# Sigmoid attention and GELU feed-forward on one core: four score tiles of a unit pair shared by VectorE and ScalarE in halves

## The chip, the cores and the metric

The kernel runs on one core of a Trainium2 chip. The metric is the device time of one launch in microseconds (us), of which three runs were made before the change. Five things work side by side on a core: TensorE (PE in the profile; its weight loads are listed apart as PEld), VectorE (DVE), ScalarE (ACT), GpSimd (POOL) and the DMA queues, most of which SyncE (SP) issues. TensorE can only write to PSUM, a small memory of eight banks; ScalarE or VectorE has to carry its results from there into SBUF before a bank can take the next ones.

## The reference

All of it is float32. Eight batches (B), twelve heads, 448 positions (S), head size 64; then a feed-forward network over the 3584 tokens with 768 and 2048 features:

```python
scores = scale * np.matmul(q, k.transpose(0, 1, 3, 2)) - np.log(S)
attn = 1.0 / (1.0 + np.exp(-scores))           # sigmoid, no softmax
x = np.matmul(attn, v)                          # then (B*S, heads*head size)
h = x @ w_in
g = 0.5 * h * (1.0 + erf(h * inv_sqrt2))
out = g @ w_out
```

## The kernel before

The first 240 us are the attention, the rest is the feed-forward network, a long unbroken row of matmuls (line L726). The change lies in the attention alone.

**Units and tiles.** The work is cut into 24 units of two head pairs (p = 0, 1) each. For each head pair the 448 keys are three full chunks of 128 (c = 0, 1, 2) and a tail of 64. A score tile (u, p, c) holds 128 keys against 448 queries for the two heads of a pair (j = 0, 1): 128 partitions by 2 x 448 numbers, each head's 448 in a PSUM bank of its own. The four PSUM places of two banks each (`ps0` to `ps3` in `place`, the order `perm`) are used in turn, so score tile n + 4 writes where score tile n was. For precision each operand is split in a high and a low float32r part (`hi`, `lo`), and a score tile takes three products (lo with hi, hi with lo, hi with hi) for two heads, six matmuls that run two at a time.

**Units in pairs.** Units 2 to 17 are done two at a time, in eight calls of `paired(u)`. Such a call first makes twelve score tiles, n = 0 to 11: 0 to 5 are those of unit u, 6 to 11 those of unit u + 1. ScalarE takes a tile out of PSUM with the sigmoid on the way (`sigmoid`, L455, 896 numbers in each partition). For n = 3 and n = 7 VectorE copies the raw scores out instead (`evict`, L459), and ScalarE does the sigmoid later, in SBUF, behind tiles 8 and 11 (`late_sigmoid`, L463). Between these copies VectorE rounds the last operand of the pair to its high part in front of tile 3 (`high_qk`, L436) and takes its low part behind tile 3 (`split_qk`, L446); tiles 9 to 11 are the first to need it.

**Values.** Then `values` multiplies the probabilities of unit u with v into a place of PSUM (`pav`, L516), tail first, then the chunks in the order of a list, once for each half of the 128 keys. In between, VectorE reads two columns of it (`mark`, L543) and TensorE makes the tail scores of the next unit (`sc_t`, L500). The same follows for unit u + 1. `park` (L575 and others) takes each result out of PSUM. VectorE and ScalarE also decode the feed-forward weights in the time between (L149, L160, L179, L187, L193).

**What sets the order.** Each engine works through its own instructions in the order in which the code above issues them; nothing is sorted anew. The tile framework adds the semaphore waits by itself, from which instruction writes or reads which tile: a matmul waits until its place in PSUM has been read, a read until its matmuls are done.

Of the kernel before, what the change touches and what calls it, by code (L numbers as in the profile page):

```python
# [14 lines left out]
AF = mybir.ActivationFunctionType  # L15
# [7 lines left out]
def tile_sigmoid_attention_gelu_ffn(  # L23
# [10 lines left out]
    nc = tc.nc  # L34
# [7 lines left out]
    FULL = S // P  # L42
# [5 lines left out]
    SCALE = 1.0 / math.sqrt(D)  # L48
    NEG_LOG_S = -math.log(S)
# [63 lines left out]
    def weight_pair(n, name):  # L113
        return sb.tile([P, 2, WU], F32R, tag=f"whl{n % 2}", name=name, bufs=WHL // 2)
# [227 lines left out]
    def rows(j):  # L342
        return slice(j * D, j * D + D)
# [20 lines left out]
    def braid(m):  # L364
        return m.rearrange("p (a b) -> p b a", a=2)
# [14 lines left out]
    def attention(at, ps):  # L380
        raws, vals, parts, probs, pavs = {}, {}, {}, {}, {}
        total = B * NU
        SINGLE = PAIRED[-1] + 2
        loaded, rounded = set(), set()
        own = at.tile([P, 8, 2, S], F32, name="a_all", bufs=1)
        lent = [wst_all[:, n * 2 * S : (n + 1) * 2 * S] for n in range(3)]
        for n in range(2):
            m = weight_pair(1, f"a_lent{n}").bitcast(F32)
# [4 lines left out]
        def occupy(u, p, c):  # L393
            slot = next(s for s in vacant if s[0] or u < SINGLE)
            vacant[:] = [s for s in vacant if s is not slot]
            probs[u, p, c] = slot
            return slot[1]

        def vacate(u, p, c):
            vacant.append(probs.pop((u, p, c)))  # L400
# [47 lines left out]
        def ordered(a):  # L448
            return a.rearrange("p j (a b) -> p j a b", a=2)

        def sigmoid(u, p, c, sc, braided):
            a = to = occupy(u, p, c)
            if braided:
                to, sc = ordered(a), sc.rearrange("p j (b a) -> p j a b", a=2)
            nc.scalar.activation(to, sc, AF.Sigmoid, bias=NEG_LOG_S, scale=SCALE)  # L455

        def evict(u, p, c, sc):
            a = occupy(u, p, c)
            nc.vector.tensor_copy(ordered(a), sc.rearrange("p j (b a) -> p j a b", a=2))  # L459

        def late_sigmoid(u, p, c):
            a = probs[u, p, c][1]
            nc.scalar.activation(a, a, AF.Sigmoid, bias=NEG_LOG_S, scale=SCALE)  # L463

        def place(i, name):
            return ps[max(i - 1, 0)].tile([P, 2, 512], F32, tag=f"ps{i}", name=name)[:, :, :S]

        def scores(u, p, c, i, finish=sigmoid):
            sc = place(i, f"sc{u}_{p}_{c}")
            keys = slice(c * P, c * P + P)  # L470
            braided = (u, p) in parts
            if braided:
                hi, lo = parts[u, p]
                terms = ((hi, lo), (lo, hi), (hi, hi))
            else:
                terms = ((raws[u][:, p],) * 2,)
            last = len(terms) - 1
            for n, (ks, qs) in enumerate(terms):
                for j in range(2):
                    nc.tensor.matmul(  # L480
                        sc[:, j],
                        ks[rows(j), 1, keys],
                        braid(qs[rows(j), 0]) if braided else qs[rows(j), 0],
                        start=n == 0,
                        stop=n == last,
                    )
            if finish is sigmoid:
                sigmoid(u, p, c, sc, braided)
            else:
                finish(u, p, c, sc)  # L490
# [18 lines left out]
        def values(u, i, tail, order, meanwhile, idle):  # L509
            pav = pavs[u] = place(i, f"pav{u}")  # L510

            def chunk(c, swap):
                a = [probs[u, 0 if c == FULL else p, c][1] for p in range(2)]
                for p, j in QUARTERS:
                    half = rows(p ^ swap)
                    nc.tensor.matmul(  # L516
                        pav[rows(j), p],
                        vals[u][half, p, j, c],
                        a[p][half, j],
                        start=not swap and c == order[0],  # L520
                        stop=c == (order[-1], FULL - 1)[swap],
                        skip_group_check=True,
                    )

            if u == total - 1:
                chunk(FULL, 0)
                for p in range(2):
                    for c in range(FULL):
                        for j in range(2):
                            nc.tensor.matmul(  # L530
                                pav[rows(j), p],
                                vals[u][:, p, j, c],
                                probs[u, p, c][1][:, j],
                                start=False,
                                stop=c == FULL - 1,
                                skip_group_check=True,
                            )
                meanwhile()
                return
            for c in order:  # L540
                chunk(c, 0)
            vacate(u, 0, FULL)
            nc.vector.tensor_copy(mark, pav[:, :, 0])  # L543
            meanwhile()
            scores_tail(u + 1, tail)
            idle()
            for c in range(FULL):
                chunk(c, 1)
            for p in range(2):
                for c in range(FULL):  # L550
                    vacate(u, p, c)
# [3 lines left out]
        def park(u):  # L555
            b, n = divmod(u, NU)
            pav = pavs[u]
            if b < 2:
# [13 lines left out]
                return  # L572
            if u < SINGLE:
                x = on_way[u % 2][:, :2]
# [17 lines left out]
        perm = (0, 1, 3, 2)  # L592
# [9 lines left out]
        def single(u):  # L602
# [11 lines left out]
            first, second = PAIRED[-1], PAIRED[-1] + 1  # L614
            if u == SINGLE:
                keep()
                dec.round(first - 2)
            if u == SINGLE + 1:
                nc.vector.tensor_tensor(x01, x11, x01, op=ALU.subtract)

            def meanwhile():
# [3 lines left out]
                if u + 1 == PAIRED[0]:  # L625
                    split_qk(u + 2, 0)
                if u == SINGLE:
                    dec.join(second - 2)
                    dec.round(second - 2)
                if u == SINGLE + 1:  # L630
                    nc.vector.tensor_tensor(kept["x6"], x01, x00, op=ALU.add)
# [22 lines left out]
        def paired(u):  # L654
            a, b, c, d = perm
            first, second = u - PAIRED[0], u + 1 - PAIRED[0]
            begun = first > 0
            after = [(u + 2, 0), (u + 2, 1)]
            if u + 2 < SINGLE:
                after.append((u + 3, 0))  # L660
            load(u + 3)
            load_v(u + 2)
            tiles = [(w, p, c) for w in (u, u + 1) for p in range(2) for c in range(FULL)]
            for n, at_tile in enumerate(tiles):
                if n == FULL:
                    high_qk(u + 1, 1, nc.vector.tensor_copy)
                scores(*at_tile, perm[n % 4], evict if n in (3, 7) else sigmoid)
                if n == 3:
                    split_qk(u + 1, 1)
                if n in (8, 11):  # L670
                    late_sigmoid(*tiles[{8: 3, 11: 7}[n]])
            part_tiles(*after[0])
            for w, p in after[1::-1]:
                high_qk(w, p, nc.gpsimd.tensor_copy)
            if begun:
                dec.round(first - 2)
                dec.join(second - 2)
                split_qk(*after[0])

            def idle1():  # L680
                load(u + 4)
                if begun:
                    dec.round(second - 2)
                    dec.post()
                else:
                    split_qk(*after[0])
                dec.scale(first)
                dec.place(first)

            values(u, a, b, [FULL, 1, 2, 0], lambda: None, idle1)  # L690
            park(u)
            load_v(u + 3)
            for w, p in after[2:]:
                high_qk(w, p, nc.gpsimd.tensor_copy)
            split_qk(*after[1])

            def idle2():
                load(u + 5)
                for w, p in after[2:]:
                    split_qk(w, p)  # L700
                dec.join(first)
                dec.scale(second)
                dec.place(second)

            values(u + 1, c, d, [0, 1, 2, FULL], lambda: None, idle2)
            park(u + 1)

        u = 0
        while u < total:
            if u in PAIRED:  # L710
                paired(u)
                a, b, c, d = perm
                perm = (b, a, d, c)
                u += 2
            else:
                single(u)
                a, b, c, d = perm
                perm = (a, b, d, c)
# [345 lines left out]
```

## Time and profile before

| | us |
|---|---|
| median of three runs (lowest, highest) | 1010.02 (1009.84, 1010.33) |
| the profiled execution | 1008.94 |
| its span, first to last instruction | 1007.0 |
| busy in the span: PE / PEld / DVE / ACT / POOL | 1002.7 / 903.0 / 719.9 / 666.0 / 127.3 |
| granted TensorE clock, share of full speed | 1.000 |

The profiled execution lies 1.94 us above its own span and 1.08 us below the median. Matmuls are pipelined, and a matmul's end in the profile is modelled: two that follow each other overlap in the list, and PE is called busy also where it came late. How far TensorE is from its own pace is seen from the distance between the starts of its matmuls, not from its busy share.

### The profile page before, as it was taken

Reading aid. Unit: us, or ns where it says so; the run is one execution under the profiler, and the core shown is the slowest. Engines: PE = TensorE matmul, PEld = TensorE weight load, DVE = VectorE, ACT = ScalarE, POOL = GpSimd, SP = SyncE. Lnnn points to the kernel's source line nnn. Section 1 sums busy time; section 2 is a strip of 40 time slices with the busy share of each in tenths; the row PEclk is TensorE's granted clock in tenths of the full one; section 3 lists DMA queues with packets and bytes.
Section 4 is the critical chain, followed back from the end, with each engine's and each line's share of the span. In section 5 each row is a group of like instructions: output and inputs, shape, how many; then the busy total and the mean of one; then the engine's idle time right before and its main releaser. Section 6 shows DMA issues by size and latency. Waiting matters only on the chain.

```text
span 1007.0 us, 16532 instructions
## 1 busy us (share of the span) xinstructions
PE 1002.7 (100%) x6406; PEld 903.0 (90%) x6406; DVE 719.9 (71%) x822; ACT 666.0 (66%) x920; POOL 127.3 (13%) x177
## 2 busy tenths in 40 slices
PE   9999999999999999999999999999999999999998
PEld 5655565567999999999999999999999999999998
DVE  3598888787988986764378877535887774378873
ACT  5787788688886766467565655766656467665652
POOL 0244444133223300010000000100000000000000
PEclk9999999999999999999999999999999999999999
DMA  9999999998997665563434546534444543334441
GB/s 247 276 278 339 361 343 346 358 321 271 344 327 215 206 219 154 168 210 132 137 110 128 151 138 183 190 110 138 126 117 147 166 150 112 112 110 126 145 142 59
DMA packets 82990, 199.16 MB, mean 198 GB/s; under 512 B 9184, under 2 KB 33984, under 8 KB 82912
## 3 DMA queue, kind: packets, MB, share of 16 engines
q1 hardware_dynamic: 69360, 152.24, 49.2%
q0 software_dynamic: 11616, 39.23, 11.4%
q10 hardware_dynamic: 1936, 6.63, 2.0%
q8 instruction: 50, 0.82, 0.3%
q14 instruction: 28, 0.23, 0.1%
HBM read 156.10 MB, written 41.29 MB: 196 GB/s over the span
## 4 chain that ended last, share of the span: by engine, by line
PE 100%; DVE 0%; ACT 0%; issue 0%
PE pf L726 76%; PE pav L516 12%; PE sc L480 9%; PE sc_t L500 2%; PE pav L530 0%; PE warm L595 0%; DVE tmp L974 0%; ACT y L975 0%
## 5 line engine op out<-in xcount | busy, mean ns | idle before, releaser
L726 PE MATMUL pf<-op,whl 128*128 128x448 f32 x2016 | 382.1, 352 | 0.0
L726 PEld LDWEIGHTS pf<-op,whl 128*128 128x128 f32 x2016 | 380.9, 189 | 0.5
L726 PE MATMUL pf<-xh_p,whl 128*128 128x448 f32 x1296 | 352.7, 353 | 0.0
L329 DVE TENSOR_TENSOR whl<-wst_all,whl 128x768 fp32r<-128x768 f32 x224 | 213.5, 954 | 153.6 <-ACT whl L322 153.2
L322 ACT CAST whl<-wst_all 128x768 fp32r<-128x768 f32 x224 | 186.0, 830 | 142.4 <-PE pf L726 124.6
L726 PEld LDWEIGHTS pf<-xh_p,whl 128*128 128x128 f32 x1296 | 244.9, 189 | 1.0 <-issue 0.7
L726 PE MATMUL pf<-xl_p,whl 128*128 128x448 f32 x624 | 219.9, 352 | 0.0
L763 DVE TENSOR_TENSOR op<-g,op 128x896 fp32r<-128x896 f32 x112 | 121.3, 1083 | 0.9 <-ACT op L773 0.9
L726 PEld LDWEIGHTS pf<-xl_p,whl 128*128 128x128 f32 x624 | 117.9, 189 | 0.1
L773 ACT CAST op<-g 128x896 fp32r<-128x896 f32 x112 | 104.8, 936 | 1.7 <-PE pf L726 1.7
L516 PE MATMUL pav<-a_all,v 64*64 64x448 f32 x936 | 104.5, 540 | 0.0
L455 ACT ACTIVATE a_all<-sc 128x896 f32<-128x896 f32 x91 | 77.0, 937 | 15.1 <-PE sc L480 15.1
L516 PEld LDWEIGHTS pav<-a_all,v 64*64 64x64 f32 x936 | 38.9, 132 | 47.4 <-issue 36.7
L763 DVE TENSOR_TENSOR g<-g,g 128x896 f32<-128x896 f32 x64 | 69.3, 1083 | 0.0
L760 ACT ACTIVATE g<-tmp 128x448 f32<-128x448 f32 x64 | 40.3, 631 | 37.8 <-DVE tmp L763 37.7
L760 ACT ACTIVATE g<-pf 128x448 f32<-128x448 f32 x64 | 34.8, 543 | 39.8 <-PE pf L726 39.6
L354 POOL DMA_DIRECT2D x<-scr_x x24 | 18.3, 816 | 324.5 <-ACT g L870 204.0
L763 DVE TENSOR_TENSOR tmp<-pf,g 128x448 f32<-128x448 f32 x64 | 39.7, 622 | 26.2 <-PE pf L726 16.6
L480 PE MATMUL sc<-lo,hi 64*128 64x448 f32 x276 | 52.5, 371 | 0.0
L446 DVE TENSOR_TENSOR lo<-qk,hi 128x896 fp32r<-128x896 f32 x46 | 51.1, 1112 | 0.9 <-POOL hi L436 0.3
L480 PE MATMUL sc<-hi,lo 64*128 64x448 f32 x276 | 49.5, 349 | 0.0
L480 PE MATMUL sc<-hi 64*128 64x448 f32 x276 | 49.5, 349 | 0.0
(87 smaller groups left out, 917.9 us busy)
## 6 DMA issues: line engine op xcount, KB each, us to landing
wst_all<-scr_in SPq DMA_DIRECT2D x112, 384.0 KB, 3.0
wst_all<-scr_out SPq DMA_DIRECT2D x112, 384.0 KB, 3.1
v<-v_dram SPq DMA_DIRECT2D x48, 256.0 KB, 10.4
raw<-w_in_dram SPq DMA_DIRECT2D x16, 767.8 KB, 8.9
out_dram<-tmp SPq DMA_DIRECT2D x47, 224.0 KB, 2.1
qk<-q_dram SPq DMA_DIRECT2D x23, 448.0 KB, 9.6
qk<-k_dram SPq DMA_DIRECT2D x46, 224.0 KB, 10.0
scr_out<-wd POOLq DMA_DIRECT2D x36, 256.0 KB, 5.0
```

What stands on the lines that cost most here:

```text
L322: nc.scalar.copy(hl[:, 0], t)
L329: nc.vector.tensor_tensor(hl[:, 1], t, hl[:, 0], op=ALU.subtract)
L354: queue.dma_start(dst[:, :, a], src[:, :, a])
L446: nc.vector.tensor_tensor(lo, raw, hi, op=ALU.subtract)
L455: nc.scalar.activation(to, sc, AF.Sigmoid, bias=NEG_LOG_S, scale=SCALE)
L480: nc.tensor.matmul(sc[:, j], ks[rows(j), 1, keys], braid(qs[rows(j), 0]) if braided else qs[rows(j), 0], start=n == 0, stop=n == last,)
L500: nc.tensor.matmul(sc[rows(p), j], raw[rows(j), p, 1, FULL * P :], raw[rows(j), p, 0], start=True, stop=True,)
L516: nc.tensor.matmul(pav[rows(j), p], vals[u][half, p, j, c], a[p][half, j], start=not swap and c == order[0], stop=c == (order[-1], FULL - ...
L726: nc.tensor.matmul(bank, a, braid(m), **flags)
L760: nc.scalar.activation(straight(dst), unbraid(src), AF.Gelu)
L763: nc.vector.tensor_tensor(out, a, b, op=op)
L773: nc.scalar.copy(op[:, 0], src)
```

## The change

In a pair, tiles 1, 3, 5 and 7 are now handled by a new function, `share`, instead of tiles 3 and 7 by `evict`. ScalarE does the sigmoid of the first head's half (448 numbers) straight from PSUM, VectorE copies the second head's half out raw, and `late_sigmoid` does only that half. The late halves of tiles 1, 3 and 5 stand behind tile 8, that of tile 7 behind tile 11. In the first `values` of a pair the chunks come in the order tail, 1, 0, 2 instead of tail, 1, 2, 0.

```diff
+        SHARED = {8: (1, 3, 5), 11: (7,)}
...
-        def evict(u, p, c, sc):
-            a = occupy(u, p, c)
-            nc.vector.tensor_copy(ordered(a), sc.rearrange("p j (b a) -> p j a b", a=2))
+        def share(u, p, c, sc):
+            a = ordered(occupy(u, p, c))
+            sc = sc.rearrange("p j (b a) -> p j a b", a=2)
+            nc.scalar.activation(a[:, 0], sc[:, 0], AF.Sigmoid, bias=NEG_LOG_S, scale=SCALE)
+            nc.vector.tensor_copy(a[:, 1], sc[:, 1])
 
         def late_sigmoid(u, p, c):
-            a = probs[u, p, c][1]
+            a = probs[u, p, c][1][:, 1]
             nc.scalar.activation(a, a, AF.Sigmoid, bias=NEG_LOG_S, scale=SCALE)
...
-                scores(*at_tile, perm[n % 4], evict if n in (3, 7) else sigmoid)
+                scores(*at_tile, perm[n % 4], share if n in SHARED[11] + SHARED[8] else sigmoid)
                 if n == 3:
                     split_qk(u + 1, 1)
-                if n in (8, 11):
-                    late_sigmoid(*tiles[{8: 3, 11: 7}[n]])
+                for m in SHARED.get(n, ()):
+                    late_sigmoid(*tiles[m])
...
-            values(u, a, b, [FULL, 1, 2, 0], lambda: None, idle1)
+            values(u, a, b, [FULL, 1, 0, 2], lambda: None, idle1)
```

VectorE's queue in the fourth pair (units 8 and 9) from `park` of the unit before to the first piece of weight decoding behind the copies (L193), with the semaphores that each instruction waits for. A score tile is named sc, unit, p, c, so `sc8_1_0` is tile 3 of this pair and `sc9_0_1` is tile 7. Before:

```order
L575 COPY h1_x_130<-pav7_1005 128x896 [waits PE_49]
L436 CAST hi9_1_1081<-qk9_796 128x896 [waits PE_49]
L459 COPY a_all_126<-sc8_1_0_1084 128x896 [waits PE_49]
L446 TENSOR_TENSOR lo9_1_1082<-qk9_796,hi9_1_1081 128x896 [waits DVE_49]
L459 COPY wst_all_109<-sc9_0_1_1117 128x896 [waits PE_49]
L193 ISA wd4_1034<-raw4_730,wd4_1034 128x1536
```

And now (`sc8_0_1` is tile 1, `sc8_1_2` tile 5; L462 is the copy in `share`, L437 and L447 are the lines that were L436 and L446):

```order
L578 COPY h1_x_130<-pav7_1023 128x896 [waits PE_49]
L462 COPY a_all_126<-sc8_0_1_1083 128x448 [waits Activation_49]
L437 CAST hi9_1_1100<-qk9_808 128x896 [waits PE_49]
L462 COPY a_all_126<-sc8_1_0_1103 128x448 [waits Activation_49]
L447 TENSOR_TENSOR lo9_1_1101<-qk9_808,hi9_1_1100 128x896 [waits DVE_49]
L462 COPY a_all_126<-sc8_1_2_1121 128x448 [waits Activation_49]
L462 COPY wst_all_109<-sc9_0_1_1138 128x448 [waits Activation_49]
L193 ISA wd4_1052<-raw4_742,wd4_1052 128x1536
```

Four half copies stand where two whole ones stood, one of them ahead of the rounding to the high part and one behind the low part. The whole copies waited for TensorE; each half copy waits for ScalarE's semaphore alone, at the count that ScalarE reaches with its own half of the same tile.

TensorE's queue in the same pair, the first matmul of tiles 5 to 9, each of which takes the PSUM place of the tile four before it. Before:

```order
L480 MATMUL sc8_1_2_1101<-lo8_1_929,hi8_1_928 128x448 [waits Activation_49]
...
L480 MATMUL sc9_0_0_1109<-lo9_0_1002,hi9_0_1001 128x448 [waits Activation_49,Pool_49]
...
L480 MATMUL sc9_0_1_1117<-lo9_0_1002,hi9_0_1001 128x448 [waits DVE_49]
...
L480 MATMUL sc9_0_2_1125<-lo9_0_1002,hi9_0_1001 128x448 [waits Activation_49]
...
L480 MATMUL sc9_1_0_1134<-lo9_1_1082,hi9_1_1081 128x448 [waits DVE_49,Activation_49]
```

And now:

```order
L483 MATMUL sc8_1_2_1121<-lo8_1_947,hi8_1_946 128x448 [waits DVE_49]
...
L483 MATMUL sc9_0_0_1130<-lo9_0_1020,hi9_0_1019 128x448 [waits Activation_49,Pool_49]
...
L483 MATMUL sc9_0_1_1138<-lo9_0_1020,hi9_0_1019 128x448 [waits DVE_49]
...
L483 MATMUL sc9_0_2_1147<-lo9_0_1020,hi9_0_1019 128x448 [waits Activation_49]
...
L483 MATMUL sc9_1_0_1158<-lo9_1_1101,hi9_1_1100 128x448 [waits DVE_49]
```

Tiles 5 and 9 (`sc8_1_2`, `sc9_1_0`) now wait for VectorE where ScalarE had cleared their place; tile 9's single wait is for the half copy of tile 5, which stands behind the low part in VectorE's queue and so covers that too. The waits of tiles 6, 7 and 8 name the same engines as before.

## Rows read from the trace of the kernel before

**Rows 1.** The page: busy us of each engine (share of the span) and instructions
```profile
PE 1002.7 (100%) x6406; PEld 903.0 (90%) x6406; DVE 719.9 (71%) x822; ACT 666.0 (66%) x920; POOL 127.3 (13%) x177
```

**Rows 2.** Waits of PE, whole span: engine, line, waited for, total, times, longest
```profile
PE warm L595 <- PEq L1054: 0.8, 1, 0.8
```

**Rows 3.** Windows, first score matmul to first value matmul: us, engines' busy us, clock, DMA
```profile
85.09:92.31 7.22, 7.22 (x76) 6.59 (x72) 6.01 (x6) 6.85 (x9) 3.36 (x3) 1.00 1.05 346
182.16:185.76 3.60, 3.60 (x40) 3.32 (x36) 3.37 (x5) 3.20 (x5) 0.73 (x1) 1.00 1.01 392
```

**Rows 4.** Timeline of PE, fourth pair: start, us, engine, line, what
```profile
88.03 0.35 PE L480 MATMUL sc<-lo,hi 64*128 64x448 f32 x2
...
88.41 0.35 PE L480 MATMUL sc<-hi 64*128 64x448 f32 x2
88.64 0.46 PE L480 MATMUL sc<-lo,hi 64*128 64x448 f32 x2
88.91 0.38 PE L480 MATMUL sc<-hi,lo 64*128 64x448 f32 x2
...
90.42 0.38 PE L480 MATMUL sc<-lo,hi 64*128 64x448 f32 x2
...
90.99 0.45 PE L480 MATMUL sc<-lo,hi 64*128 64x448 f32 x2
91.28 0.35 PE L480 MATMUL sc<-hi,lo 64*128 64x448 f32 x2
...
92.31 0.61 PE L516 MATMUL pav<-a_all,v 64*64 64x448 f32 x4
```

**Rows 5.** Timeline of PEld, fourth pair, the weight loads of tile 6
```profile
88.61 0.21 PEld L480 LDWEIGHTS sc<-lo,hi 64*128 64x128 f32 x2 [0.20 <-issue]
88.72 0.22 PEld L480 LDWEIGHTS sc<-hi,lo 64*128 64x128 f32 x2
```

**Rows 6.** Timeline of ACT, fourth pair: the sigmoids of tiles 1 and 4
```profile
86.78 0.91 ACT L455 ACTIVATE a_all<-sc 128x896 f32<-128x896 f32 x1
...
88.37 0.94 ACT L455 ACTIVATE a_all<-sc 128x896 f32<-128x896 f32 x1
```

**Rows 7.** Timeline of DVE, fourth pair
```profile
87.10 0.70 DVE L436 CAST hi<-qk 128x896 fp32r<-128x896 f32 x1 [0.77 <-PE sc L480]
87.72 1.07 DVE L459 COPY a_all<-sc 128x896 f32<-128x896 f32 x1
88.71 1.07 DVE L446 TENSOR_TENSOR lo<-qk,hi 128x896 fp32r<-128x896 f32 x1
```

**Rows 8.** Groups by line and shape, whole span: busy us, mean ns of one, idle before
```profile
L760 ACT ACTIVATE g<-pf 128x448 f32<-128x448 f32 x64 | 34.8, 543 | 39.8 <-PE pf L726 39.6
L760 ACT ACTIVATE g<-tmp 128x448 f32<-128x448 f32 x64 | 40.3, 631 | 37.8 <-DVE tmp L763 37.7
L580 DVE COPY x<-pav 128x448 f32<-128x448 f32 x12 | 6.9, 618 | 4.1 <-PE pav L530 3.8 <-PE pav L516 0.4
```

**Rows 9.** Timelines of DVE and ACT: two such instructions back to back, PSUM to SBUF
```profile
231.43 1.16 DVE L580 COPY x<-pav 128x448 f32<-128x448 f32 x2
...
244.07 0.96 ACT L870 COPY g<-pf 128x448 f32<-128x448 f32 x2
```

**Rows 10.** Timelines of ACT and DVE: an instruction of VectorE that waits for ScalarE's
```profile
601.74 0.83 ACT L322 CAST whl<-wst_all 128x768 fp32r<-128x768 f32 x1 [1.73 <-PE pf L726]
602.61 0.96 DVE L329 TENSOR_TENSOR whl<-wst_all,whl 128x768 fp32r<-128x768 f32 x1 [1.45 <-ACT whl L322]
```

**Rows 11.** Timelines of DVE and PEld: a weight load that waits for VectorE
```profile
101.63 0.16 DVE L543 COPY ones<-pav 128x2 f32<-128x2 f32 x1 [0.87 <-PE pav L516]
101.84 0.13 PEld L516 LDWEIGHTS pav<-wst_all,v 64*64 64x64 f32 x1 [0.31 <-DVE ones L543]
```

**Rows 12.** Timeline, end of the program: the last PSUM tile, read in halves
```profile
1003.53 0.39 DVE L974 COPY tmp<-pf 128x224 f32<-128x224 f32 x1 [7.28 <-PE pf L726]
...
1003.96 0.35 ACT L975 COPY y<-pf 128x224 f32<-128x224 f32 x1 [1.03 <-DVE tmp L974]
```

## The prediction, made before the changed kernel was run

> **What bounds the kernel now.** First the page's busy line: TensorE is busy 100% of the span [rows 1]. Then its waits: one, of 0.8 us, at the start [rows 2]. By these two nothing can be gained or lost outside TensorE, but a matmul that comes late is still counted busy, so the third view is a comparison of stretches by the windows [rows 3]. The twelve score tiles of a pair take 7.22 us from the first score matmul to the first value matmul; the six of a single unit take 3.60 us. Matmul pairs of one kind follow at 0.189 us ((90.42 - 88.91)/8, [rows 4]), so six more tiles of three pairs should cost 18 x 0.189 = 3.40 us, and the pair 7.00 us. 0.22 us are lost in a pair.
>
> The fourth view, the starts of the matmuls, shows where [rows 4]. Tile 6 begins at 88.64, 0.23 after the pair of matmuls before it, and 0.27 pass to its second pair: 0.50 where two steps are 0.38. Tile 10 begins on time at 90.99, but its second pair follows after 0.29 instead of 0.19. Both take the place of a tile that ScalarE reads late (tile 2, tile 6): it needs 0.795 us a tile ((88.37 - 86.78)/2 for tiles 1, 2 and 4, [rows 6]) and TensorE 3 x 0.189 = 0.567, and VectorE's two tiles do not quite make up for it. In the weight loads the wait is seen as a late start at 88.61; a matmul runs 0.11 us after its weight load has begun (the next load starts at 88.72, the next matmul, one step later, at 88.91, [rows 4, 5]). Everything else in a pair is TensorE's own pace, so what a pair's score tiles gain or lose reaches the end of the program whole.
>
> **The change, step by step.** I follow VectorE's queue of the fourth pair; the other seven have the same steps. Three things that the trace of before doesn't show have to be bounded.
>
> *Halves on ScalarE.* A sigmoid of 448 numbers out of PSUM isn't in the trace. The nearest row is the GELU from `pf` in the same shape, 0.54 us; the dearest of that shape is the one from `tmp`, 0.63 [rows 8]. I take 0.54. Two copies of that shape take 0.96 together [rows 9], so the next one starts 0.42 after. Per pair ScalarE gives up two whole sigmoids in PSUM order and two late ones (4 x 0.795 = 3.2) and gets eight halves (8 x 0.42 = 3.4): near nothing, and hidden, since it idles in the values.
>
> *Halves on VectorE.* A copy of 448 out of PSUM takes 0.62 [rows 8], two take 1.16, so the next starts after 0.54 [rows 9]. Two wholes (each 0.99 to the next, 87.72 to 88.71, [rows 7]) become four halves, 2.16 against 1.98. By volume nothing is moved.
>
> *The new wait.* Each half copy waits for ScalarE, which reaches that count with its half of the same tile, as the order of the changed kernel shows. The halves are thus not read side by side but one after the other. The trace has this once, at the end of the program: ScalarE starts its half at 1003.96, when VectorE's ends at 1003.92 [rows 12]. From ScalarE's end to VectorE's start 0.04 pass (601.74 + 0.83 = 602.57 to 602.61, [rows 10]).
>
> Now the queue, from ScalarE's tile 1, which starts at 86.78 in either kernel, as nothing before it changes:
> - half of tile 1 on ScalarE 86.78 to 87.32; VectorE's half from 87.36, next instruction 87.90.
> - rounding to the high part at 87.90. Before it began at 87.10; it is stuck behind a copy that waits. Its successor can start 0.62 later (87.10 to 87.72, [rows 7]), 88.52.
> - ScalarE: tile 2 at 86.78 + 0.42 = 87.20, half of tile 3 at 88.00, done at 88.54. VectorE's half of tile 3 from max(88.52, 88.58) = 88.58 (before 87.72), next at 89.12.
> - the low part at 89.12 (before 88.71). It takes 1.07 and, like the copy ahead of it (1.07, next after 0.99), lets the next one start at 90.11.
> - half of tile 5 on VectorE 90.11 to 90.73, though ScalarE's half is done about 89.8.
> - TensorE's tile 9 needs that place, and the low part. From VectorE's end to a weight load 0.05 pass (101.79 to 101.84, [rows 11]), 0.11 more to the matmul: 90.73 + 0.16 = 90.89.
>
> Tile 9 began at 90.42 before [rows 4], so it comes 0.47 later. Smaller waits before it (tile 5 for the half of tile 1: 87.36 + 0.62 + 0.16 = 88.14 against 88.03; tile 7 for that of tile 3, some 0.1) lie inside this, since tile 9's start is set by VectorE's queue and not by TensorE's. Behind tile 9 the wait at tile 10 goes (ScalarE has finished tile 6 by 90.6, and tile 10 is due at 91.46): 0.10 back. Tile 11's place is free at about 91.9, and it is due at 92.0. So the values begin at 92.31 + 0.47 - 0.10 = 92.68, that is 0.37 us later, and with eight pairs 8 x 0.37 = 3.0 us.
>
> *What costs nothing.* The late halves of tiles 1, 3 and 5 start after tile 8 on ScalarE, about 91.7, and are done before 93.3; with the new order of chunks tile 1's is asked for first, after the tail chunk, about 93.4, and the others later still. Tile 9's sigmoid comes some 0.7 later than now; its place is wanted by the tail scores, 3 us after the values begin. If that cover were gone, each late half would cost up to 0.54. VectorE's decoding behind the copies slides by 0.5, the column read that frees the second half of the values by as much as TensorE itself. The rest of the program moves as a whole.
>
> The profiled execution, 1008.94, would become 1011.9, and the median, 1.08 above it, 1010.02 + 3.0 = 1013.0 us.
>
> *Bounds.* With ScalarE's half at 0.63 and 0.52 to the next, 0.1 enters at tile 3 from the sigmoid and 0.1 from its later start: 0.57 a pair, 4.6 us, 1014.6. If copies and low part run tightest (0.02 less in each of six steps), 0.25 a pair, 1012.0. A gain from the halves themselves is excluded by the wait, as long as the built order runs as it stands.
>
> **Rivals.**
>
> *The halves run side by side and ScalarE's backlog is gone.* In favour: VectorE and ScalarE do read different tiles out of PSUM at once at normal durations (VectorE's tile 3 at 87.72 and ScalarE's tile 4 at 88.37, [rows 6, 7]). Against: the wait above. Without it VectorE's half of tile 1 would run at 86.6, the rounding at 87.1 as now, the low part at about 88.3, the half of tile 5 end at about 89.9, and tile 9 be free at 90.1, before 90.3, when it is due without any wait. All 0.22 would be won: 8 x 0.22 = 1.8 us, 1008.2. This ends on the other side; it decides if VectorE's half of tile 5 is done by 90.14. The Trainium skill's page "PSUM — Partial Sum Buffer" (Specifications (TRN2)) speaks for this outcome: it says that both engines can read PSUM at once at full bandwidth as long as no bank collides, and the two heads lie in two banks. No run here shows two engines in one tile at once, and rows 12 show them in turn.
>
> *The delay is taken up later in the pair.* The first step of the scores and that into the values are each about 0.1 longer than 0.189; if these were waits for something that VectorE's delay doesn't move, 0.2 of the 0.37 would vanish: 8 x 0.17 = 1.4 us, 1011.4. Against: the single unit's 3.60 holds the same two steps, with no such queue behind them.
>
> *ScalarE becomes the bound too.* If a half costs 0.63 and each VectorE start waits longer than 0.04, say 0.15, tile 3's half, tile 5's and tile 7's slip: about 0.7 a pair, 5.6 us, 1015.6. Against: the copies of 448 out of PSUM in rows 9.
>
> **Numbers.** Forecast (1012.0 to 1014.6) 0.75; side by side (1008.2) 0.07; taken up later (about 1011.4) 0.13; dearer (1015.6) 0.05. 0.2%, 2.0 us, is what a measurement of this kernel can tell from no change. The gain of 1.8 lies just within, so faster gets 0.04; the same gets the rest of that case, the taken-up one and the low edge of the forecast, 0.20; slower 0.76. The range for 8 in 10 runs from 1011.2, which takes in most of the taken-up case, to 1014.6, its upper bound; the likeliest case's own range is 1012.0 to 1014.6.
>
> **What would show it.** Right: in the fourth pair VectorE's first half copy starts just behind ScalarE's half of tile 1, about 87.4, the rounding near 87.9, the low part near 89.1; tile 9 late, about 90.9, with a weight load that starts after VectorE's fourth instruction; tile 10 without a wait; 7.6 us from the first score matmul to the first value matmul in all eight pairs, and no change elsewhere. Wrong: half copies that overlap ScalarE's half of the same tile, a rounding still at 87.1, or a score stretch of 7.0 to 7.2.

## The result, and the profile after

The changed kernel takes 1016.51 us (median of six runs, 1016.29 to 1016.76), where the kernel before, timed beside it, takes 1009.93 (1008.73 to 1010.74, six runs). The ratio is 1.0067, with a 95% interval of 1.0054 to 1.0080. It is slower, as forecast, but by 6.6 us instead of 3.0, and outside the range. The profiled execution took 1016.61 us, its span is 1014.8, 7.8 more than before. The medians differ by less than the spans, as the profiled execution of the kernel before lay 1.0 under its median and that of the changed kernel 0.1 above.

The page's busy line has moved hardly at all, apart from GpSimd (POOL), whose busy time fell by 6.0 us:

```profile
PE 1004.9 (99%) x6406; PEld 901.4 (89%) x6406; DVE 722.4 (71%) x838; ACT 668.1 (66%) x952; POOL 121.3 (12%) x177
```

TensorE's waits answer to [rows 2]. A wait that was not there now stands first: seven times in a program of eight pairs. The columns are engine, line, what it waited for, total, times, longest.

```profile
PE sc L483 <- DVE a_all L462: 5.5, 7, 0.8
```

The windows from the first score matmul to the first value matmul answer to [rows 3]. The first line is the first pair, the second the fourth:

```profile
26.40:34.02 7.62, 7.49 (x77) 6.49 (x74) 5.23 (x10) 6.75 (x12) 0.58 (x1) 1.00 1.04 288
...
87.31:95.59 8.28, 7.50 (x78) 6.50 (x74) 7.02 (x9) 7.90 (x14) 2.87 (x4) 1.00 1.04 332
```

Measured the same way over all pairs, the stretch was 7.23 us eight times before; now it is 7.62 in the first pair and 8.27 in the seven others. That is 0.39 + 7 x 1.04 = 7.7 us, of the 7.8 by which the span grew. The other stretches of the attention moved by less than 0.04 us each, except the very first, at the program's start, which differs from run to run (4.97 to 5.59 us over all traces here) and is 0.3 shorter in this one. The feed-forward part is 0.5 longer (766.97 against 766.50), but that isn't the change: in x1 and x7, whose score stretches are as long as here, it is 766.5 again. So the first pair costs what the forecast asked of every pair (0.37), and the others cost 0.65 more. VectorE's queue in the fourth pair shows where (answering to [rows 7]; start, us, engine, line, what):

```profile
89.57 0.63 DVE L462 COPY a_all<-sc 128x448 f32<-128x448 f32 x1 [1.01 <-ACT a_all L461]
90.11 0.62 DVE L437 CAST hi<-qk 128x896 fp32r<-128x896 f32 x1
90.82 0.62 DVE L462 COPY a_all<-sc 128x448 f32<-128x448 f32 x1
91.36 1.73 DVE L447 TENSOR_TENSOR lo<-qk,hi 128x896 fp32r<-128x896 f32 x1
93.02 0.61 DVE L462 COPY a_all<-sc 128x448 f32<-128x448 f32 x1
93.55 0.61 DVE L462 COPY wst_all<-sc 128x448 f32<-128x448 f32 x1
```

The pair begins at 87.31 instead of 85.09, so 2.22 comes off for a comparison with the forecast: the half of tile 1 at 87.35 (forecast 87.36), the rounding at 87.89 (87.90), the half of tile 3 at 88.60 (88.58), the low part at 89.14 (89.12). All as forecast, to 0.02 us. But the low part takes 1.73 us instead of 1.07 [rows 7], and the half of tile 5 begins at 90.80, not at 90.11. TensorE's tile 9 waits for it. Its weight load is the second line below and starts 0.05 after VectorE's 93.02 + 0.61; the first line is tile 7, which waits for the half of tile 3 as forecast:

```profile
91.50 0.19 PEld L483 LDWEIGHTS sc<-lo,hi 64*128 64x128 f32 x2 [0.19 <-DVE a_all L462]
...
93.68 0.18 PEld L483 LDWEIGHTS sc<-lo,hi 64*128 64x128 f32 x2 [1.13 <-DVE a_all L462]
```

What runs beside the low part is on GpSimd. Its queue in the fourth pair, after the change:

```profile
91.22 0.93 POOL L437 CAST hi<-qk 128x896 fp32r<-128x896 f32 x1 [1.62 <-PE sc L483]
93.04 0.93 POOL L437 CAST hi<-qk 128x896 fp32r<-128x896 f32 x1 [0.89 <-PE sc L483]
```

and the same two casts in the kernel before, of which the forecast had shown and used nothing:

```profile
88.90 1.69 POOL L436 CAST hi<-qk 128x896 fp32r<-128x896 f32 x1 [1.53 <-PE sc L480]
90.75 0.93 POOL L436 CAST hi<-qk 128x896 fp32r<-128x896 f32 x1 [0.16 <-PE sc L480]
```

These casts round operands of the next units; the code issues them behind the twelve score tiles, but GpSimd does them as soon as TensorE is done with the score tiles that they wait for. Before, VectorE's low part began at 88.71 [rows 7], 0.19 us ahead of the first cast, and the cast paid: 1.69 us instead of the 0.93 of its twin. Now the low part begins 0.14 us behind the cast, and the low part pays: 1.73 instead of 1.07, while the cast takes its 0.93. On GpSimd, where nothing in the stretch waits for these casts, the collision had cost nothing; in VectorE's queue it costs 0.65 us, which tile 9 waits out. The trace of before even held the case with VectorE as the loser: its decoding behind the copies began inside the second cast and took 1.40 us, where the next of its kind took 0.95.

```profile
91.09 1.40 DVE L193 CUSTOM_DVE_ANT_0 wd<-raw,wd 128x1536 uint16<-128x1536 uint16 x1
...
95.70 0.95 DVE L193 CUSTOM_DVE_ANT_0 wd<-raw,wd 128x1536 uint16<-128x1536 uint16 x1
```

The first pair of the same execution is the counter-example. VectorE:

```profile
30.44 1.08 DVE L447 TENSOR_TENSOR lo<-qk,hi 128x896 fp32r<-128x896 f32 x1
31.44 0.62 DVE L462 COPY a_all<-sc 128x448 f32<-128x448 f32 x1
```

GpSimd, whose casts there still wait for data from DRAM and start when the stretch is over (34.02):

```profile
34.73 1.81 POOL L437 CAST hi<-qk 128x896 fp32r<-128x896 f32 x2 [6.90 <-DMA qk<-k_dram]
```

No cast, no slow low part, and 7.62 us.

The Trainium skill has this as a rule: the page "SBUF — State Buffer" (SBUF: two separate sides) says that VectorE and GpSimd share one pair of SBUF ports, that an instruction of VectorE with two SBUF inputs needs it against a GpSimd instruction that reads SBUF, and that whichever starts first holds it for its whole length while the other stands still. The low part has two SBUF inputs (`qk` and `hi`) and the cast reads SBUF. The trace agrees to 0.13 us: the cast ends at 91.22 + 0.93 = 92.15, a low part that starts only then would end at 93.22, and it ends at 93.09; before, the low part ended at 89.78 and the cast at 90.59, 0.81 later, where a whole one is 0.93.

### The profile page after: what moved, and what is told of

Its sections match the earlier page's. It is cut to its first block, busy times and chain, and to the rows that moved or that the text cites. A ratio compares the mean times of both kernels' runs of the same rounds, so it can differ in the third digit from the quotient of the medians.

```text
span 1014.8 us, 16565 instructions
## 1 busy us (share of the span) xinstructions
PE 1004.9 (99%) x6406; PEld 901.4 (89%) x6406; DVE 722.4 (71%) x838; ACT 668.1 (66%) x952; POOL 121.3 (12%) x177
## 4 chain that ended last, share of the span: by engine, by line
PE 90%; DVE 4%; ACT 2%; issue 2%; DMA 0%; POOL 0%; DVEq 0%; POOLq 0%
PE pf L729 70%; PE pav L519 12%; PE sc L483 5%; PE sc_t L503 2%; ACT a_all L456 1%; DVE lo L447 1%; DVE a_all L462 1%; ACT a_all L461 1%; DVE tmp L766 1%; DMA scr_out<-wd 0%; DVE whl L329 0%; PE pav L533 0%; PE warm L598 0%; POOL scr_out L221 0%; DVE wd L179 0%
## 5 line engine op out<-in xcount | busy, mean ns | idle before, releaser
L456 ACT ACTIVATE a_all<-sc 128x896 f32<-128x896 f32 x75 | 66.2, 943 | 14.9 <-PE sc L483 14.9
L447 DVE TENSOR_TENSOR lo<-qk,hi 128x896 fp32r<-128x896 f32 x46 | 55.8, 1212 | 0.6
L456 ACT ACTIVATE a_all<-sc_t 128x896 f32<-128x896 f32 x24 | 22.0, 918 | 45.3 <-PE sc_t L503 45.3
```

Of the source, the lines that this page charges most:

```text
L447: nc.vector.tensor_tensor(lo, raw, hi, op=ALU.subtract)
```

## The experiments

The theory from the traces: two causes. The two halves of a tile are read in turn, which costs 0.39 us in each pair (forecast); and in seven pairs the cast that has begun first holds the low part up, 0.65 us more (not forecast). The main rivals: the low part is slow for another reason (ScalarE's or VectorE's half reads beside it), or the 1.04 us belong to the halves as such. The first four ran beside a kernel before of 1009.42 us (median of 25 runs), the last three beside one of 1009.53 (13 runs).

**GpSimd's casts in the other order** (`x1_pool_later`), meant to bring the cast that runs beside the low part later:

```diff
-            for w, p in after[1::-1]:
+            for w, p in after[:2]:
                 high_qk(w, p, nc.gpsimd.tensor_copy)
```

> The changed kernel, but GpSimd rounds the two parts of the next pair in the other order: first the part whose buffer comes free only after score tile 8, so that none of its casts runs while VectorE makes the low part (lo, L447) in the score stretch. Theory (GpSimd's cast, begun 0.14 us ahead of the low part, holds VectorE up): lo takes 1.07 us instead of 1.73, the score stretch is 7.6 us in all eight pairs instead of 7.62 in the first and 8.27 in seven, and the time falls by 7 x 0.65 = 4.6 us against the changed kernel, to about 3 us above the kernel before. Rival (the low part is slow because of the half copies and half sigmoids around it, or of where its operands lie): lo stays at 1.73, the stretch at 8.27, the time as the changed kernel.

1016.56 us, ratio 1.0068 (1.0052 to 1.0085). A miss, because the edit did not do what it should: in the fourth pair, which begins at 87.93, a cast still starts at 91.84, 3.91 us into the stretch as in the changed kernel (91.22 - 87.31), and the low part at 91.98 still takes 1.73.

```profile
91.98 1.73 DVE L447 TENSOR_TENSOR lo<-qk,hi 128x896 fp32r<-128x896 f32 x1
```

```profile
91.84 0.93 POOL L437 CAST hi<-qk 128x896 fp32r<-128x896 f32 x1 [1.63 <-PE sc L483]
```

In either order the cast issued first starts at the same place, when TensorE is done with a score tile, so the time tells the theories apart in nothing. One pair of this run does say something. In the third, which begins at 67.53, the cast begins 3.85 us into the stretch instead of 3.91, and the low part at the same 4.05. The low part takes 1.67 instead of 1.73, and the stretch 8.21 instead of 8.27:

```profile
71.38 0.93 POOL L437 CAST hi<-qk 128x896 fp32r<-128x896 f32 x1 [7.34 <-PE sc L483]
```

```profile
71.58 1.67 DVE L447 TENSOR_TENSOR lo<-qk,hi 128x896 fp32r<-128x896 f32 x1
```

**The kernel before, with GpSimd made to begin first** (`x2_pool_first`): two more copies on GpSimd behind VectorE's rounding to the high part, whose result the first one reads; the second has 1536 numbers. Nothing of the change is in it.

```diff
+                    spare = weight_pair(0, f"spare{u}").bitcast(F32).rearrange("p a b -> p (a b)")
+                    nc.gpsimd.tensor_copy(spare[:, :2], parts[u + 1, 1][0].bitcast(F32)[:, 0, :2])
+                    nc.gpsimd.tensor_copy(spare, raws[u + 1].rearrange("p a b s -> p (a b s)")[:, : 2 * WU])
```

> The kernel before, plus one extra GpSimd copy per pair (1536 numbers, SBUF to SBUF, result unused) that starts when VectorE's cast to the high part is done, at about 87.9 in the fourth pair, and so ahead of the low part at 88.71. Theory (whichever of the two starts first keeps the other waiting): the copy runs about 1.6 us, the low part, 1.07 before, is listed with 1.7 to 1.9 and ends near 90.5, tile 9 comes 0.3 late, the stretch is 7.4 instead of 7.22 and the time 1 to 2 us above the kernel before. Rival (the changed kernel's halves slow the low part): it stays at 1.07, stretch 7.22, time as before.

1011.33 us, ratio 1.0019 (1.0010 to 1.0028). In the fourth pair the low part of the kernel before is slow too, once GpSimd has begun ahead of it:

```profile
89.72 1.87 DVE L446 TENSOR_TENSOR lo<-qk,hi 128x896 fp32r<-128x896 f32 x1
```

```profile
89.18 1.46 POOL L671 COPY spare<-qk 128x1536 f32<-128x1536 f32 x1
```

1.87 instead of 1.07; the copy ends at 90.64, and the low part 0.95 us after that. No half is read here, so the slow low part isn't a thing of the halves. The price is smaller than in the changed kernel, 7.40 to 7.55 us a stretch. By the queues that is because tile 9 needs the low part here, but no copy behind it: the place that it writes is read by ScalarE.

**The changed kernel with VectorE's half first** (`x3_dve_first`): the two lines of `share` change places, so ScalarE's half waits for VectorE's.

```diff
-            nc.scalar.activation(a[:, 0], sc[:, 0], AF.Sigmoid, bias=NEG_LOG_S, scale=SCALE)
             nc.vector.tensor_copy(a[:, 1], sc[:, 1])
+            nc.scalar.activation(a[:, 0], sc[:, 0], AF.Sigmoid, bias=NEG_LOG_S, scale=SCALE)
```

> The changed kernel with the two halves of share issued in the other order: VectorE's copy first, ScalarE's half behind it. ScalarE's half now waits for VectorE's. Theory (the turn-taking costs on whichever engine waits, and the low part, back near 88.3, is ahead of GpSimd's cast): lo 1.07 to 1.09, GpSimd's cast 1.6; ScalarE's queue loses about 0.4 by the first half and 0.3 more by that of tile 5, tiles 6, 9 and 10 come late; stretch about 7.6, time about 3 us above the kernel before and 4.6 below the changed one. Rival (only GpSimd's cast costs anything, the turn-taking nothing): stretch 7.0 to 7.2, time as before or up to 1.8 below.

1011.81 us, ratio 1.0023 (1.0013 to 1.0032); stretches of 7.51 to 7.58 us. The low part is 0.65 us ahead of the cast again and takes its normal time, though the same eight half reads stand around it:

```profile
87.43 0.62 DVE L461 COPY a_all<-sc 128x448 f32<-128x448 f32 x1 [0.20 <-PE sc L483]
...
89.14 1.07 DVE L447 TENSOR_TENSOR lo<-qk,hi 128x896 fp32r<-128x896 f32 x1
```

```profile
89.79 1.22 POOL L437 CAST hi<-qk 128x896 fp32r<-128x896 f32 x1 [1.52 <-PE sc L483]
```

ScalarE now has the wait that VectorE had, and 0.28 to 0.35 us of the 1.04 remain in a pair; the halves still go in turn. That the order of two lines turns the wait round shows that it comes from the way the program is built: the later reader of a PSUM tile waits for the earlier one.

```profile
88.09 0.55 ACT L462 ACTIVATE a_all<-sc 128x448 f32<-128x448 f32 x1 [0.31 <-DVE a_all L461]
```

**No turn-taking** (`x4_half_tiles`): every PSUM place is two tiles of one bank each, so that a half waits for its matmuls alone. All sigmoids become halves by this, those of the single units too, and each `park` and `mark` becomes two instructions. The diff below is the heart of a longer one:

```diff
-            return ps[max(i - 1, 0)].tile([P, 2, 512], F32, tag=f"ps{i}", name=name)[:, :, :S]
+            pool = ps[max(i - 1, 0)]
+            return [pool.tile([P, 512], F32, tag=f"ps{i}{j}", name=f"{name}{j}")[:, :S] for j in range(2)]
```

> The changed kernel with every PSUM place cut into two tiles of one bank, one per head, so that VectorE's half copy waits for TensorE alone. Every whole sigmoid, park and mark becomes two instructions of half the size. Theory (the order of the two halves comes from their being one PSUM tile, and side by side they take away ScalarE's backlog): VectorE's half of tile 1 starts with ScalarE's, near 86.6, the low part near 88.3 with 1.07, GpSimd pays; the stretch is 7.0 to 7.2 (a whole sigmoid costs ScalarE 0.84 in two halves instead of 0.795, which may keep 0.1), time 0 to 1.8 us below the kernel before. Rival (two engines reading one tile's banks at once slow each other, or the halves as such cost): copies over 0.7 us, stretch 7.4 or more.

1010.72 us, ratio 1.0010 (1.0001 to 1.0020). VectorE's half of tile 1 begins at 86.73, ScalarE's at 86.99, and neither is longer for it; the stretch is 7.16 us in all eight pairs, 0.07 less than before the change:

```profile
86.73 0.62 DVE L463 COPY a_all<-sc 128x448 f32<-128x448 f32 x1 [0.17 <-PE sc L485]
...
88.47 1.08 DVE L447 TENSOR_TENSOR lo<-qk,hi 128x896 fp32r<-128x896 f32 x1
```

```profile
86.99 0.55 ACT L462 ACTIVATE a_all<-sc 128x448 f32<-128x448 f32 x1
```

```profile
85.26:92.42 7.16, 7.16 (x76) 6.83 (x73) 6.79 (x10) 6.85 (x16) 3.60 (x4) 1.00 1.03 370
```

So the 0.39 us are the wait between the halves and not the halves themselves. The kernel as a whole gains nothing, because five of the six single units became 0.37 us longer from start to start. In the first of them ScalarE's twelve half sigmoids take that much longer than six whole ones (the first line is x4's, the last that of the kernel before), and the last value matmuls wait for them (the middle line):

```profile
182.86 5.34 ACT L458 ACTIVATE a_all<-sc 128x448 f32<-128x448 f32 x12 [0.34 <-PE sc L485]
```

```profile
188.26 0.20 PEld L521 LDWEIGHTS pav<-a_all,v 64*64 64x64 f32 x6 [0.22 <-ACT a_all L458]
```

```profile
183.04 4.97 ACT L455 ACTIVATE a_all<-sc 128x896 f32<-128x896 f32 x6 [0.40 <-PE sc L480]
```

**The changed kernel with GpSimd held back** (`x5_pool_waits`), the test that x1 had missed: at tile 8 GpSimd copies two numbers of the late half of tile 7, so its casts wait until VectorE is past the low part. The half reads and their turns stay.

```diff
+                if n == 8:
+                    nc.gpsimd.tensor_copy(ones[:, 4:6], probs[tiles[7]][1][:, 1, :2])
```

> The changed kernel with one addition: in each pair, at the ninth score tile, GpSimd copies two numbers of the late half of tile 7, so that its casts of q and k wait until VectorE's half copy of tile 7, which stands behind the low part in VectorE's queue, is done. Theory (the changed kernel loses 0.39 us a pair because the half copies wait in turn, and 0.65 more in seven pairs because GpSimd's cast begins before VectorE's low part and slows it from 1.08 to 1.73 us): the low part takes 1.07 to 1.10 us in all eight pairs, the score stretch is 7.6 us in all of them as it is now in the first, and the time falls by 7 x 0.65 = 4.6 us, to about 1012.0, some 2.5 to 3 above the kernel before. Rival (the low part is slow for another reason, such as the half copies or ScalarE's reads beside it): the low part stays at 1.73, the stretch at 8.27 and the time at 1016.5.

1013.71 us, ratio 1.0041 (1.0026 to 1.0056). The stretch is 7.62 us in all eight pairs, which now all look like the first one of the changed kernel. The fourth, as window, VectorE and GpSimd:

```profile
87.03:94.65 7.62, 7.49 (x76) 6.49 (x72) 6.08 (x10) 7.26 (x13) 1.66 (x3) 1.00 1.05 337
```

```profile
91.08 1.08 DVE L447 TENSOR_TENSOR lo<-qk,hi 128x896 fp32r<-128x896 f32 x1
92.08 0.62 DVE L462 COPY a_all<-sc 128x448 f32<-128x448 f32 x1
```

```profile
93.73 0.84 POOL L674 COPY ones<-wst_all 128x2 f32<-128x2 f32 x1 [4.43 <-DVE wst_all L462]
94.51 2.89 POOL L437 CAST hi<-qk 128x896 fp32r<-128x896 f32 x2
```

The 0.65 us are gone from seven pairs, 4.5 us, and the rival is out. The time fell by less, 2.8 us: outside the score stretches the attention became 1.9 us longer, 0.19 us in the first tail scores of seven pairs and 0.05 in the values behind them, and once 0.24, in the second tail scores of the second pair. The trace shows what is late: the two casts, now beside VectorE's decoding, take 2.89 us, VectorE's next low part waits for them, the column read that frees the second half of the values (`mark`, L546) stands behind it, and TensorE waits for that. The expectation had left this out.

```profile
97.44 1.09 DVE L447 TENSOR_TENSOR lo<-qk,hi 128x896 fp32r<-128x896 f32 x1 [0.83 <-POOL hi L437]
98.45 0.15 DVE L546 COPY ones<-pav 128x2 f32<-128x2 f32 x1
```

```profile
98.65 0.21 PEld L519 LDWEIGHTS pav<-a_all,v 64*64 64x64 f32 x8 [0.79 <-DVE ones L546]
```

**The control: the kernel before with GpSimd held back** (`x6_before_pool_waits`), the same two lines.

> The control to the run beside it: the kernel before with the same two-number copy on GpSimd at the ninth score tile (there it waits for the whole copy of tile 7). Theory: the low part starts ahead of GpSimd's cast anyway, so it keeps its 1.07 us and the stretch its 7.23, GpSimd's first cast loses its 1.69 us for about 0.93 to 1.2, and the time is that of the kernel before, within 0.5 us. Rival (holding GpSimd back is a gain or a loss by itself, whatever the low part does): the stretch or the rest of the pair moves, and the time by more than 1 us.

1010.36 us, ratio 1.0007 (0.9997 to 1.0016). The stretch stays at 7.23 us in all pairs and the low part at 1.08: where the low part was ahead of the cast anyway, holding the cast back gives nothing. Outside the stretches 0.8 us are added, in the same places as in x5. The fourth pair:

```profile
85.48:92.71 7.23, 7.23 (x77) 6.60 (x73) 6.06 (x8) 6.88 (x9) 1.39 (x3) 1.00 1.04 367
```

```profile
89.09 1.08 DVE L446 TENSOR_TENSOR lo<-qk,hi 128x896 fp32r<-128x896 f32 x1
```

**The old order of the chunks** (`x7_old_order`):

```diff
-            values(u, a, b, [FULL, 1, 0, 2], lambda: None, idle1)
+            values(u, a, b, [FULL, 1, 2, 0], lambda: None, idle1)
```

> The changed kernel with the chunks of the value matmuls in the order that they had in the kernel before. Theory: the order of the chunks costs nothing, as the late halves are done before their chunks are asked for in either order: 1016.5 as the changed kernel, within 0.5 us, stretches of 7.62 and 8.27, and the rest of the pair unchanged. Rival (the late halves are asked for too early in the old order, so the new one hides a loss): the values of a pair take over 0.1 us longer, 0.8 us or more in all.

1016.37 us, ratio 1.0066 (1.0051 to 1.0081), and no stretch of the attention, bar the first, moved by 0.04 us against the changed kernel. The order costs and brings nothing.

No version came out that beats the kernel before. One-bank tiles in the pairs alone, with whole ones in the single units, might keep the 0.07 us a pair, 8 x 0.07 = 0.6 us by x4; that is less than these runs can tell from nothing, and it wasn't tried.

## Where the prediction was right, and where it failed

**Right: what bounds.** TensorE's matmuls that come late are the whole story; no other engine's busy time counts. The 7.7 us of the score stretches reach the end of the program whole.

**Right: the new wait and its price.** VectorE's half begins behind ScalarE's half of the same tile. The queue's first four starts hold to 0.02 us, the halves cost what the nearest rows said (0.62 on VectorE, 0.54 to 0.62 on ScalarE), and the price per pair, forecast as 0.37, is 0.39 wherever this wait acts alone: in the first pair and in all eight of x5. Tile 10 has no wait, as forecast.

**Failed: the low part.** The step reads: the low part "takes 1.07 and, like the copy ahead of it (1.07, next after 0.99), lets the next one start at 90.11". It takes 1.73 in seven of eight pairs, and the next one starts at 90.80 on the same scale. The duration was taken from a row in which the low part was the first of two that collide, and was kept for a place in time at which it is the second. It had been slid by 0.41 us in VectorE's queue (88.71 to 89.12), and what stands between these times on the other engines was left out: GpSimd's cast at 88.90, which begins when TensorE is done with a score tile and so slides by only 0.10 (91.22 - 2.22 = 89.00). The 1.69 us of that cast, against 0.93 of the next, had said that the two collide and who pays. By the rows of before the cast still had 88.90 + 0.93 - 89.12 = 0.71 us to go when the low part was due. With the 0.65 that was measured, the sum would have been 0.37 + 0.65 in the seven pairs whose casts aren't late, some 7.5 us and 1017.5, against 1016.51 measured. That "the other seven have the same steps" failed with it: the first pair has no cast in its stretch, before and after.

**The bounds** were those of the new wait alone, 0.25 to 0.57 us a pair. They were right for it (0.39), and too narrow for the whole, as no other term was open.

**The rivals.** Side by side: not in this kernel, but x4 shows that it is the built order that excludes it; the two halves in two banks are read at once at 0.62 and 0.55 us, as the Trainium skill's page "PSUM — Partial Sum Buffer" (Specifications (TRN2)) has it. Even so, 0.07 us a pair are won and not the 0.22 that the rival gave: tile 9 comes without a wait, but the first value matmul, which takes the place of tile 8, then waits for ScalarE's sigmoid of that tile:

```profile
92.42 0.21 PEld L521 LDWEIGHTS pav<-a_all,v 64*64 64x64 f32 x8 [0.28 <-ACT wst_all L458]
```

Taken up later: no; all of the delay arrived. ScalarE as the bound: its time (1015.6) is the nearest of all, yet its mechanism isn't there. VectorE's first half starts 0.03 us after ScalarE's end, not 0.15, and ScalarE's halves follow at 0.43:

```profile
89.00 0.54 ACT L461 ACTIVATE a_all<-sc 128x448 f32<-128x448 f32 x1
89.43 0.93 ACT L456 ACTIVATE a_all<-sc 128x896 f32<-128x896 f32 x1
90.22 0.56 ACT L461 ACTIVATE a_all<-sc 128x448 f32<-128x448 f32 x1
```

**What costs nothing** was right throughout: the three late halves run in one piece from 93.88 to 95.46 and are done as the values begin (95.58), VectorE's decoding slides without a price, and the chunks' order is free (x7).

```profile
93.88 1.58 ACT L466 ACTIVATE a_all<-a_all 128x448 f32<-128x448 f32 x3
```

## What to carry to other kernels

A duration read from a trace belongs to its neighbours in time as much as to its instruction: whoever slides an instruction has to look at what the other engines do at its new place, GpSimd above all when the instruction is VectorE's with two inputs from SBUF, and an instruction that takes far longer than its twin (1.69 against 0.93) marks a collision whose cost can change sides. Two engines share one PSUM tile only in turn if the program orders them by tiles; to read at once they need tiles of their own. And when a delay shows in seven of eight equal places, the eighth is a free experiment.

## What was not expected of the hardware

0.33 us between the starts of two instructions (0.19 ahead to 0.14 behind) decides which of VectorE's low part and GpSimd's cast is held up. The price is the same for either: what is left of the one that began first, less 0.12 to 0.14 us. The rows above give it five times:

| began first | left of it when the other begins | the other takes, alone takes | lost |
|---|---|---|---|
| low part (kernel before) | 89.78 - 88.90 = 0.88 | cast 1.69, 0.93 | 0.76 |
| cast (changed kernel) | 92.15 - 91.36 = 0.79 | low part 1.73, 1.07 | 0.66 |
| GpSimd's copy (x2) | 90.64 - 89.72 = 0.92 | low part 1.87, 1.07 | 0.80 |
| low part (x3) | 90.21 - 89.79 = 0.42 | cast 1.22, 0.93 | 0.29 |
| second cast (kernel before) | 91.68 - 91.09 = 0.59 | decoding 1.40, 0.95 | 0.45 |
